# One issuing queue instead of two: a fused linear-attention and MLP-mixer kernel whose loads and stores move to SyncE, with a new issue order for every engine

## The chip, the cores and the metric

The kernel runs on one core of one Trainium2 chip. The metric is the device time of one execution in microseconds. Five engines take part: TensorE (PE in the profile; its weight loads are shown as PEld), VectorE (DVE), ScalarE (ACT), GpSimd (POOL) and SyncE (SP). SP computes nothing here; it issues transfers. ACT can issue transfers too, on a queue of its own, in order with its computing instructions.

## The reference

```python
def _attn_ref(q, k, v, alpha):               # (4, 8, 768, 48) each
    state = np.zeros((B, H, D, D))
    for t in range(S):
        state = alpha[:, :, t, :, None] * state + np.einsum('bhd,bhe->bhde', k[:, :, t], v[:, :, t])
        y[:, :, t] = np.einsum('bhd,bhde->bhe', q[:, :, t], state)
    return y

def _moe_ref(x, w_tok1, w_tok2, w_ch1, w_ch2):   # x = y with the heads side by side: (4, 768, 384)
    h = np.maximum(x.transpose(0, 2, 1) @ w_tok1, 0.0) @ w_tok2
    u = x + h.transpose(0, 2, 1)
    return u + np.maximum(u @ w_ch1, 0.0) @ w_ch2
```

Per batch element, a gated recurrence over 768 steps and 8 heads gives a 768 x 384 matrix x. A mixer follows: one MLP over the steps (768 to 256 to 768), then one over the channels (384 to 1536 to 384), both with residuals. Input and output are float32; the kernel multiplies in bfloat16.

## The kernel before

**Attention.** The 4 batch elements have 3 pieces each, so there are 12 pieces, n = 0 to 11, of 256 steps. A piece needs four loads of 384 KB (`ld_at`, `ld_kt`, `ld_qt`, `ld_vt`, line 533) into a pool of 20 buffers named `in`. ACT takes logarithms of alpha (`ln`, lines 580 to 586), PE sums them over time (`cum`, `cumw`), ACT exponentiates (`E`, `IE`), and `kk` and `qq` (line 641) scale keys and queries on DVE or POOL. Pieces 0 to 5 transpose keys and queries on PE (`trk`, `trq`, line 654) and copy them out (`evk`, `evq`). Pieces 6 to 11 send them through a transposing transfer (`dk`, `dq`, line 665, issued by SP) and reorder the query part (`pq`). `G` and `mask` (line 708) form masked scores, `K`, `sa` and `sm` update the state, `y` and `ia`, `ib` give the piece's output, `x` (line 685 or 686) copies it out. `kc` and `vs` are half-tile copies between these; `kc` of a late piece waits for `dk`.

**Mixer.** For each batch element b, `t1` and `t2` (lines 790, 795) are the MLP over steps with `ht` as its activation, `u` (line 799) adds the residual, `up`/`ut` or, for b = 2 and 3, the transposing transfer `ux` (line 669) turn u, `c1` (line 814) and the activation `rt` (lines 785, 787) are the first channel product, `c2` (line 819) the second, `o` (line 823) adds the residual and `st` (line 573) stores 192 KB. Weights come in 16 pieces of 384 KB (`ldw`), and `cw` casts each to bfloat16.

**Fillers.** In the first pieces, PE multiplies zeros where it would wait (`f1_...` one, `f3_...` three matmuls of 512 columns, line 592).

**Order.** Nothing is scheduled on the chip or by a framework. `ORDER` lists all 942 operations with the engine that runs each as the last letter (t PE, s ACT, v DVE, g POOL, y SP), and `BUFS` gives every value its buffer. Each engine works through its own operations in the listed order and waits at each one for its operands. In the built program every transfer also uses one of eight completion counters in turn, for both queues together, and waits until the transfer that used the same counter before it has landed.

**What the change touches.** The operands of `cum` in `attention`, the two column ranges in which the last output tile is made (`cuts` in `mixer`, for batch 3, tile 0), and the two lists.

Of the kernel before, what the change touches and what calls it, by code (L numbers as in the profile page):

```python
# [368 lines left out]
G1_1t evq2s ib1t ldw_wt21s f3_trk2t kk2v E3s IE3s trk2t sm1_1g mask1_1v vb2s vs1_1s f1_K2t ld_vt3y K2t evk2v G1_2t
ldw_wt20y y1_1t ld_at4y sa0_2v f3_G02t kk3g x1_0s r13s sm0_2g q0r3g G0_2t mask1_2v vs0_2g cw_wt10s ia1t x0_0v y0_1t  # L370
trk3t t1_0_1_0t mask0_2v ka3s ia2t ldw_wc14y t1_0_1_1t f1_y2t ib2t y0_2t vs1_2v kb3s ldw_wc15y y1_2t x1_1s cw_wt11s
vb3v x0_1s t1_0_1_2t t1_0_0_0t t1_0_1_3t kc3s x0_2s t1_0_1_4t vs0_3v vs1_3v ldw_wc13y x1_2s t1_0_0_1t qq3v cw_wt21s
t1_0_0_2t t1_0_1_5t cw_wt20v t1_0_0_3t t1_0_0_4t t1_0_0_5t ht_0_1s K3t trq3t ld_kt4y ht_0_0s P4g s0_3v sa1_3v t2_0_2t
t2_0_3t evk3s sm1_3g t2_0_0t t2_0_1t t2_0_5t ldw_wc12y ldw_wc10y ldw_wc11y u_0_3v u_0_2v u_0_0v up_0_1t t2_0_4t evq3s
lnP4s cw_wc14g cw_wc15g u_0_1v ib3t ut_0_1s ln14s ld_kt5s u_0_5v cw_wc13g up_0_0t cum4t ld_at5y E4s G0_3t IE4s u_0_4v
G1_3t k0a4g ut_0_0v up_0_2t c1_0_10_0t mask0_3v c1_0_9_0t ut_0_2s rt_0_10_0s rt_0_9_0s mask1_3v c1_0_7_0t c1_0_9_1t
c1_0_6_0t c1_0_10_1t c1_0_8_0t c1_0_8_1t cw_wc12s y1_3t cw_wc10s rt_0_10_1s kk4v rt_0_7_0v cw_wc11v rt_0_6_0v trk4t
c1_0_1_0t P5g ka4g c1_0_4_1t rt_0_8_1v c1_0_1_1t k0a5g ld_vt4s r14s x1_3s c1_0_3_1t c1_0_0_0t evk4v rt_0_1_1v
# [5 lines left out]
sa1_4v rt_0_7_1s c2_0_2_0t kc5s cw_wc22s c2_0_1_0t trq5t c2_0_4_0t vb5g cw_wc24g ib4t c2_0_4_1t y1_4t c2_0_1_1t
ld_at7s evq5s ld_vt6s cw_wc23s sm1_4g vs1_5g x1_4v P6g G0_5t G1_5t ld_kt6y vs0_5s cw_wc25s ld_kt7s mask1_5v c2_0_2_1t
ln16s mask0_5v c2_0_4_2t c2_0_2_2t c2_0_1_2t K5t y0_3t sa0_5v c2_0_4_3t c2_0_1_3t o_0_4v c2_0_5_0t r16s x0_3s lnP6s
ia5t y0_5t sm0_5v ld_at8y x0_5s ld_qt6y cum6t ld_at9y IE6s t1_1_0_0t E6s ib5t t1_1_0_1t st_0_4y y1_5t ld_vt7y x1_5s
t1_1_0_2t t1_1_1_0t t1_1_0_3t t1_1_1_1t t1_1_0_4t t1_1_1_2t t1_1_1_3t t1_1_1_4t t1_1_0_5t c2_0_5_1t k0a6g o_0_1v kk6v
dk6y P7g ka6g t1_1_1_5t c2_0_5_2t c2_0_0_0t ln18s ht_1_1s lnP7s vb6s ht_1_0v t2_1_3t t2_1_2t P8v q0r6v t2_1_5t
c2_0_5_3t t2_1_0t t2_1_1t st_0_1s u_1_2v u_1_3v qq6g k0a7g u_1_5v ld_qt7y u_1_0v cum7t IE7s kb6s t2_1_4t up_1_1t ln17s  # L390
vs0_6s ld_qt8y ld_at10s c2_0_3_0t c2_0_3_1t u_1_4v u_1_1v c2_0_0_1t up_1_0t c2_0_3_2t ut_1_1v o_0_5v up_1_2t c2_0_2_3t
c2_0_3_3t ut_1_0v kk7v c1_1_1_0t kc6v ut_1_2v vs1_6s lnP8s vb7s P9g K6t r17s c2_0_0_2t c2_0_0_3t rt_1_1_0v dq6y
c1_1_0_0t ld_kt8y q0r7g o_0_2v ld_qt9s E7s o_0_3v qq7g dk7y cum8t ln19s lnP9s E8s r19s r18s s0_6v sa1_6v c1_1_11_0t
c1_1_3_0t c1_1_2_0t o_0_0v vs0_7s rt_1_11_0v c1_1_3_1t c1_1_7_1t kb7g ka7s rt_1_3_1s c1_1_4_1t rt_1_2_0v ld_kt9y
c1_1_0_1t c1_1_10_1t rt_1_3_0s q0r8v dq7y c1_1_1_1t rt_1_0_1s P10v rt_1_7_1v rt_1_10_1v c1_1_11_1t sm1_6g pq6g
c1_1_7_0t cum9t lnP10s IE8s rt_1_1_1s vs1_7s c1_1_8_1t c1_1_4_0t ld_vt8s ln110s rt_1_7_0v ld_at11y rt_1_11_1s
c1_1_2_1t c1_1_9_1t qq8v k0a8v rt_1_8_1s rt_1_4_1s c1_1_5_0t rt_1_0_0v rt_1_9_1v q0r9g rt_1_4_0s ld_vt9y rt_1_2_1s
IE9s c1_1_5_1t rt_1_5_0v kc7s E9s c1_1_6_1t dq8y rt_1_5_1s K7t ld_qt10y c1_1_6_0t G0_6t rt_1_6_1s k0a9v rt_1_6_0s
r110s pq7s G1_6t sa0_7v mask0_6v kk8g c2_1_4_0t mask1_6v dk8y c2_1_4_1t sm0_7g c2_1_4_2t sa1_7v kk9g ib6t st_0_5s
st_0_0s c1_1_9_0t c2_1_4_3t P11g qq9g rt_1_9_0s y1_6t G1_7t G0_7t mask0_7v x1_6s c1_1_8_0t c2_1_1_0t c1_1_10_0t vb9s  # L400
ka9s rt_1_8_0v y0_6t ia7t mask1_7v vb8v y0_7t rt_1_10_0s c2_1_3_0t c2_1_1_1t q0r10v sm1_7v x0_6s vs1_8v c2_1_0_0t
c2_1_3_1t c2_1_3_2t ib7t pq8s t1_2_1_0t x0_7s vs0_8g kc8g y1_7t c2_1_3_3t o_1_4v dk9y kb9g ld_kt10y cum10t o_1_3v
vs0_9s x1_7s G0_8t E10s t1_2_1_1t IE10s ln111s vs1_9s qq10g mask0_8v K8t c2_1_1_2t r111s dq9y sa0_8v sm0_8g ia8t
t1_2_1_2t t1_2_1_3t G1_8t c2_1_0_1t y0_8t kc9s K9t c2_1_1_3t mask1_8v x0_8s lnP11s st_1_4y st_0_2y ld_kt11y pq9s
k0a10v kk10g ld_vt10y ld_qt11y s0_9v sa1_9v t1_2_0_0t c2_1_0_2t ib8t y1_8t c2_1_0_3t t1_2_0_1t t1_2_1_4t t1_2_0_2t
t1_2_0_3t t1_2_0_4t x1_8v o_1_1v t1_2_1_5t ht_2_1s G0_9t o_1_0v G1_9t t1_2_0_5t ht_2_0s mask0_9v c2_1_2_0t dq10y ib9t
c2_1_2_1t t2_2_5t t2_2_3t cum11t mask1_9v y0_9t u_2_5v u_2_3v t2_2_4t t2_2_2t t2_2_0t u_2_4v pq10s t2_2_1t x0_9s ka10s
k0a11g sm1_9g u_2_2v vb10v vs1_10g u_2_1v c2_1_5_0t c2_1_2_2t c2_1_5_1t dk10y c2_1_5_2t y1_9t ia10t kb10v vs0_10g
# [469 lines left out]
```

## Time and profile before

| | |
|---|---|
| three runs | 166.69, 167.17 (median), 168.16 us |
| profiled execution | 167.49 us, of which its span (first to last instruction) 165.8 us |
| busy: PE, DVE, ACT, POOL | 155.9, 117.6, 102.6, 65.3 us |
| transfers | 25.17 MB read, 4.72 MB written; SP's queue (q1) 25.47 MB, ACT's (q10) 8.75 MB |
| transfers issued by SP, by ACT | 76, 29 |

The span is cut into engines and waits by several views. A row of a timeline or of a list of groups names the line of the code, the engine, the operation, output and input, and how many of them (x); "busy, mean ns" belongs to the group; what stands behind an arrow released the wait ahead of it. A row of a table of windows gives, for one stretch of the span, the busy time of each engine, the granted clock, the mean busy share of the transfer engines and the GB/s that they moved. PE's busy time holds modelled ends of pipelined matmuls, so a full PE may still have room.

### The profile page before, as it was taken

The numbers are of one execution on the slowest core, as the hardware profiler recorded it, in microseconds if no ns is written. First come the engines' busy times: TensorE is split into PE (matmuls) and PEld (weight loads), VectorE is DVE, ScalarE is ACT, GpSimd is POOL, SyncE is SP. The second block draws the span as 40 slices with busy tenths as digits, with TensorE's granted clock in tenths as the row PEclk, the third lists the DMA queues.
The fourth block names the chain that finished last, engine by engine and source line by source line (L and its number), as shares of the span: only waits on it lengthen the run. The fifth ranks groups of instructions, "written<-read, shape, count | busy, mean of one in ns | idle before, by whom it ended". The sixth has DMA issues, their size and how long they took to land. (4 is left out here: it accounts for less than half of the span.)

```text
span 165.8 us, 4057 instructions
## 1 busy us (share of the span) xinstructions
PE 155.9 (94%) x1606; PEld 99.2 (60%) x1606; DVE 117.6 (71%) x205; ACT 102.6 (62%) x195; POOL 65.3 (39%) x73
## 2 busy tenths in 40 slices
...
GB/s 116 323 325 324 320 325 369 373 321 335 368 353 315 204 298 208 271 264 190 303 237 129 241 270 144 142 134 163 185 0 51 0 90 100 47 190 4 47 95 142
DMA packets 74530, 34.46 MB, mean 208 GB/s; under 512 B 67984, under 2 KB 73488, under 8 KB 74512
## 3 DMA queue, kind: packets, MB, share of 16 engines
q1 hardware_dynamic: 58432, 25.47, 60.4%
q10 hardware_dynamic: 16080, 8.75, 17.9%
...
HBM read 25.17 MB, written 4.72 MB: 180 GB/s over the span
## 5 line engine op out<-in xcount | busy, mean ns | idle before, releaser
L819 PE MATMUL ps<-wc,rt 128*128 128x384 bf16 (+1 forms) x300 | 53.9, 320 | 0.0
L814 PE MATMUL ps<-ut,wc 128*128 128x384 bf16 x288 | 51.4, 326 | 1.7 <-ACT rt L785 1.6
L785 ACT ACTIVATE rt<-ps 128x384 bf16<-128x384 f32 x59 | 26.7, 490 | 21.4 <-PE ps L814 19.2
L814 PEld LDWEIGHTS <-wc 128*128 128x128 bf16 x288 | 27.3, 97 | 19.4 <-issue 2.4
L819 PEld LDWEIGHTS <-rt 128*128 128x128 bf16 x300 | 27.5, 97 | 15.5
L708 DVE TENSOR_TENSOR gtm<-ps,mk 128x1024 bf16<-128x1024 f32 x24 | 28.6, 1219 | 3.9 <-PE ps L592 3.5
L787 DVE TENSOR_SCALAR rt<-ps 128x384 bf16<-128x384 f32 x37 | 19.9, 554 | 11.0 <-PE ps L814 10.9
L823 DVE TENSOR_TENSOR o<-ps,u 128x384 f32<-128x384 f32 (+1 forms) x25 | 13.1, 536 | 11.8 <-PE ps L819 9.0
L641 POOL TENSOR_TENSOR pkk<-in,IE 128x768 bf16<-128x768 f32 x7 | 12.7, 1816 | 16.3 <-DVE pkk L641 7.7
L641 POOL TENSOR_TENSOR pkq<-in,E 128x768 bf16<-128x768 f32 x7 | 12.7, 1819 | 3.2 <-DVE ss L756 1.5
L592 PE MATMUL ps<-zs 128*128 128x512 bf16 x37 | 12.3, 454 | 1.6 <-DVE zs L495 1.1
L685 ACT CAST vb<-in 64x384 bf16<-64x384 f32 (+1 forms) x20 | 12.4, 621 | 1.1 <-DMA in<-in_v_dram 0.8
L685 ACT CAST x<-ps 128x384 bf16<-128x384 f32 x18 | 8.5, 476 | 7.4 <-PE ps L592 6.9
L799 DVE TENSOR_TENSOR u<-ps,x 128x384 bf16<-128x384 f32 x24 | 11.9, 550 | 1.3 <-PE ps L795 1.0
L756 POOL TENSOR_TENSOR ss<-tmp,E 128x384 bf16<-128x384 f32 x10 | 8.3, 835 | 7.8 <-DVE tmp L753 4.6
L577 POOL TENSOR_TENSOR in<-in 128x384 f32<-128x384 f32 x7 | 7.0, 1000 | 11.1 <-DVE wt L686 3.4
L790 PE MATMUL ps<-x,wt 128*128 128x384 bf16 x48 | 10.8, 326 | 0.3 <-ACT x L685 0.3
L753 DVE TENSOR_TENSOR tmp<-ps,ss 128x384 f32<-128x384 f32 x16 | 8.8, 553 | 2.0 <-PE ps L592 1.3
L641 DVE TENSOR_TENSOR pkk<-in,IE 128x768 bf16<-128x768 f32 x5 | 4.8, 954 | 7.1 <-ACT IE L625 6.0
L592 PE MATMUL ps<-tpq,tpk 48*64 48x128 bf16 (+1 forms) x288 | 8.5, 219 | 1.0 <-DVE tpq L686 0.8
L795 PE MATMUL ps<-ht,wt 128*128 128x384 bf16 x48 | 9.3, 326 | 0.0
L592 PEld LDWEIGHTS <-gtm 128*128 128x128 bf16 x192 | 7.6, 96 | 1.9
...
## 6 DMA issues: line engine op xcount, KB each, us to landing
in<-in_q_dram SPq DMA_DIRECT2D x11, 384.0 KB, 5.1
in<-in_moe_w_ch_dram SPq DMA_DIRECT2D x10, 384.0 KB, 5.9
in<-in_alpha_dram SPq DMA_DIRECT2D x9, 384.0 KB, 5.8
in<-in_k_dram SPq DMA_DIRECT2D x9, 384.0 KB, 6.4
in<-in_v_dram SPq DMA_DIRECT2D x6, 384.0 KB, 5.5
in<-in_v_dram ACTq DMA_DIRECT2D x6, 384.0 KB, 5.7
out_dram<-o ACTq DMA_DIRECT2D x12, 192.0 KB, 2.6
out_dram<-o SPq DMA_DIRECT2D x11, 192.0 KB, 2.3
```

What stands on the lines that cost most here:

```text
L592: return self.pe.matmul(out, lhsT=lhsT, rhs=rhs, start=start, stop=stop, skip_group_check=True)
L641: self.shared(self.eng[e].tensor_tensor(self.t(dst)[:, :, :, 0:D], self.t(src).rearrange("p h s d -> p s h d"), bass.AP(tensor=f.tensor, o ...
L685: return self.act.copy(d, s)
L708: self.nc.vector.tensor_tensor(self.t(gtm)[:, hf, :, :], self.pair(gp).rearrange("p a (j t) -> p (a j) t", t=128), bass.AP(tensor=m.tensor ...
L785: self.act.activation(d, s, AF.Relu)
L787: self.nc.vector.tensor_scalar_max(d, s, 0.0)
L790: self.pe.matmul(self.bank(bank)[:, 0:HD], lhsT=self.wt1[:, kc, m * 128 : m * 128 + 128], rhs=self.t(x), start=(kc == 0), stop=(kc == NS - 1))
L795: self.pe.matmul(self.bank(bank)[:, 0:HD], lhsT=self.wt2[:, kc, i * 128 : i * 128 + 128], rhs=self.t(hts[kc]), start=(kc == 0), stop=(kc = ...
L799: self.nc.vector.tensor_tensor(self.t(u)[:, i % 3], self.bank(bank)[:, 0:HD], self.t(x), ALU.add)
L814: self.pe.matmul(self.bank(bank)[:, 0:HD], lhsT=self.wc1[:, kc, mc * 128 : mc * 128 + 128], rhs=self.t(ut)[:, 3 * half : 3 * half + 3, kc, ...
L819: self.pe.matmul(self.bank(bank)[:, 0 : cz - ca], lhsT=self.t(rts[mc][0])[:, i * 128 : i * 128 + 128], rhs=self.wc2[:, mc, ca:cz], start=( ...
L823: self.nc.vector.tensor_tensor(self.t(o)[:, ca:cz], self.bank(bank)[:, 0 : cz - ca], self.t(u)[:, i % 3, ca:cz], ALU.add)
```

## The change

Three edits. `cum` gets the filler operations of `fill("cumw", cb)` as predecessors (`fill` returns an empty list for n of 3 and more, and this branch is taken for n of 3 and more alone). The last output tile is cut at column 320 instead of 192. And `ORDER` and `BUFS` are replaced: every load is issued by SP, and all stores but four of the last batch (`st_3_1`, `st_3_3`, `st_3_4`, `st_3_0h1`). SP then issues 101 transfers and ACT 4. The order within every engine is new, 155 operations change engine, DVE has 186 operations instead of 187, ACT 189 instead of 223, POOL 71 instead of 61. PE keeps the same operations and 37 filler matmuls, in another order.

```diff
-            cum = O("cum", pe([384] + [4] * 4 + [16]), 2, writes=[cb, E, IE], reads=[la], preds=[lnp], emit=lambda e: g.cum(cb, la))
+            cum = O("cum", pe([384] + [4] * 4 + [16]), 2, writes=[cb, E, IE], reads=[la], preds=[lnp] + fill("cumw", cb),
+                    emit=lambda e: g.cum(cb, la))
...
-            cuts = [(0, HD // 2), (HD // 2, HD)] if (b, i) == LAST else [(0, HD)]
+            cuts = [(0, 320), (320, HD)] if (b, i) == LAST else [(0, HD)]
...
 ORDER = """
-f1_cumw0t ld_at1y f3_cumw1t f3_trk1t ld_at0s ld_kt1s f1_cumw1t ln1s f3_trq0t ld_kt0y ld_vt0y ld_qt0y ln0s ld_vt1y
-ld_qt1y ld_at2y cumw1t f1_K1t cumw0t ld_at3y E1s IE1s Et1s IE0s vb0s f1_K0t kk0v Et0s kk1g K0t f3_K1t s0_0v sa1_0v E0s
-qq0v vb1s trk0t sm1_0v f3_G00t trq0t ln2s trk1t evk0v ld_qt2y qq1g K1t evq0v evk1s sa0_1v ld_vt2s G0_0t cumw2t
...
-rt_0_9_1s c1_0_11_1t q0r4v qq4v c1_0_4_0t ld_vt5s rt_0_1_0s rt_0_2_0v E5s c1_0_2_1t rt_0_4_0s rt_0_11_1s kk5g
...
-c2_3_5_3t c2_3_0h0_1t o_3_5v c2_3_0h1_0t c2_3_0h1_1t c2_3_0h1_2t c2_3_0h1_3t st_3_5s o_3_0h1v st_3_4y c2_3_0h0_2t
-c2_3_0h0_3t o_3_0h0v st_3_0h0y st_3_0h1s
+f3_cumw0t f3_K0t f3_cumw1t ld_at1y ln1s f1_cumw0t ld_at0y f3_trk0t cumw1t ld_kt0y ld_vt0y ld_qt0y ln0s cumw0t f1_trq0t
+f3_trq0t E1s IE0s kk0v Et0s E0s IE1s Et1s trk0t vb0v qq0g K0t f3_G00t ld_kt1y ld_vt1y s0_0v sa1_0v f3_K1t trq0t kk1v
+sm1_0v vb1s ld_qt1y vs1_0s f1_K1t ld_at3y ld_at2y ld_kt2y evq0v K1t ln13s evk0v trk1t sa0_1v qq1g ld_qt2y G0_0t vs0_0s
...
+c2_3_0h0_0t o_3_4v c2_3_3_3t st_3_1s o_3_3v st_3_4s c2_3_0h1_3t o_3_0h1v c2_3_0h0_1t c2_3_0h0_2t c2_3_0h0_3t o_3_0h0v
+st_3_0h0y st_3_3s st_3_0h1s
...
```

Two stretches of the new lists, engine by engine. DVE from its first working operation to the first `u`:

```
before  kk0 s0_0 sa1_0 qq0 sm1_0 evk0 evq0 sa0_1 mask0_0 sa1_1 evq1 mask1_0 mask0_1 kk2 mask1_1 evk2 sa0_2 mask1_2 x0_0 mask0_2 vs1_2 vb3 vs0_3 vs1_3 qq3 cw_wt20 s0_3 sa1_3 u_0_3
after   kk0 vb0 s0_0 sa1_0 kk1 sm1_0 evq0 evk0 sa0_1 mask0_0 sa1_1 evq1 mask1_0 mask0_1 kk2 cw_wt10 mask1_1 evk2 sa0_2 kk3 mask1_2 mask0_2 qq3 x1_2 evk3 s0_3 ht_0_1 sa1_3 u_0_2
```

SP's queue around the last piece, n = 11, and POOL's:

```
SP before    dq9 st_1_4 st_0_2 ld_kt11 ld_vt10 ld_qt11 dq10 dk10 ux_2_1 st_1_0 ux_2_0 dq11 dk11
SP after     dq9 st_1_4 ld_qt11 ld_vt10 dq10 dk10 ld_kt11 ux_2_1 st_0_3 ux_2_0 st_1_1 ld_vt11 dq11 dk11
POOL before  qq10 sm0_8 kk10 k0a11 sm1_9 vs1_10 vs0_10 kk11 pq11 sm0_11
POOL after   qq10 sm0_8 kk10 sm1_9 vb10 kb10 pq10 kc10 vs0_10 k0a11 kk11 q0r11 sm0_10 kc11 vs0_11 pq11 sm0_11
```

More of the change, by code (lines that the diff above doesn't have):

```diff
@@ L369 @@
[L369 to L378, printed above, removed]
@@ L384 @@
[L384 to L393, printed above, removed]
@@ L394 @@
[L394 to L408, printed above, removed]
@@ new lines @@
+ld_kt3y ld_qt3y ld_vt3y lnP3s Et2s IE2s sm1_1g qq2g mask1_0v mask0_1v cum3t ldw_wt11y f1_y0t ib0t G1_1t y1_0t y0_0t
+ia1t kk2v IE3s f1_trq2t vs1_1s ld_at4y E3s x1_0s cw_wt10v y0_1t vb2s f1_trk2t mask1_1v k0a3g ldw_wt20y ldw_wt21y trq2t
+f3_trk2t ldw_wc14y ldw_wc13y evq2s trk2t evk2v K2t f3_G02t x0_0s sa0_2v ib1t G1_2t x0_1s vs0_2s q0r3g ldw_wc15y kk3v
+sm0_2g vb3s y1_1t vs1_2g ka3g kb3s vs1_3s t1_0_0_0t t1_0_0_1t G0_2t trk3t t1_0_1_0t mask1_2v t1_0_0_2t mask0_2v ia2t
+t1_0_1_1t t1_0_1_2t f1_y2t ib2t qq3v vs0_3s cw_wt11s ld_at5y y0_2t y1_2t kc3s x1_1s ldw_wc10y x0_2s t1_0_0_3t
@@ new lines @@
+t1_0_1_3t t1_0_1_4t x1_2v K3t P4g cw_wt21g evk3v s0_3v cw_wt20s lnP4s t1_0_1_5t t1_0_0_4t t1_0_0_5t cw_wc14g trq3t
+ht_0_0s ht_0_1v cum4t sa1_3v ln14s ldw_wc11y cw_wc15g cw_wc13g E4s evq3s t2_0_2t u_0_2v t2_0_3t P5g t2_0_0t t2_0_4t
+u_0_3v ldw_wc12y t2_0_1t u_0_0v up_0_1t IE4s ut_0_1s ld_kt4y ld_qt4y t2_0_5t ib3t u_0_1v up_0_0t ut_0_0s G0_3t u_0_4v
+G1_3t u_0_5v up_0_2t ut_0_2s mask0_3v c1_0_9_0t c1_0_10_0t ld_vt4y ld_kt5y cw_wc10v c1_0_8_0t mask1_3v rt_0_9_0s
+rt_0_10_0v c1_0_9_1t c1_0_8_1t rt_0_8_1v sm1_3g cw_wc11g r14s cw_wc12s c1_0_6_0t c1_0_11_1t ln15s y1_3t c1_0_4_1t
@@ new lines @@
+rt_0_8_0v ldw_wc20y ld_qt5y ldw_wc21y rt_0_6_0s x1_3s k0a4v rt_0_11_1s kk4v q0r4v c1_0_7_0t rt_0_7_0v c1_0_3_0t
+ldw_wc22y lnP5s c1_0_2_1t c1_0_1_1t ka4g rt_0_3_0s rt_0_4_1s kb4s rt_0_9_1s qq4v c1_0_3_1t c1_0_10_1t cum5t ldw_wc25y
+ld_vt5y vb4g trk4t k0a5g vs0_4g ldw_wc23y rt_0_1_1s c1_0_1_0t trq4t c1_0_4_0t rt_0_3_1s IE5s E5s kc4s r15s vs1_4s
+ldw_wc24y rt_0_10_1v evk4v rt_0_1_0s ld_at7y c1_0_2_0t rt_0_2_1v rt_0_4_0v ld_at6y kk5v c1_0_0_0t evq4s c1_0_0_1t
+rt_0_0_1s c1_0_5_0t trk5t G1_4t rt_0_2_0v G0_4t rt_0_0_0v rt_0_5_0s mask0_4v evk5s cw_wc20s mask1_4v ld_vt6y ld_at8y
@@ new lines @@
+cum10t c2_1_1_3t G1_8t G0_8t o_1_1v mask0_8v E10s IE10s vs1_8s c2_1_0_0t c2_1_0_1t vs1_9g ln111s kc9s vs0_9s pq9s
+qq10g sm0_8g kk10g ia8t c2_1_0_2t mask1_8v y0_8t t1_2_1_0t t1_2_1_1t K9t x0_8v s0_9v c2_1_0_3t ib8t t1_2_0_0t
+t1_2_0_1t y1_8t t1_2_1_2t sa1_9v G0_9t ld_vt10y x1_8s G1_9t mask0_9v t1_2_1_3t t1_2_0_2t mask1_9v t1_2_0_3t t1_2_0_4t
+t1_2_0_5t ht_2_0s dq10y t1_2_1_4t t1_2_1_5t cum11t sm1_9g ht_2_1s c2_1_2_0t y0_9t t2_2_3t t2_2_4t t2_2_1t u_2_3v
+t2_2_5t vb10g kb10g u_2_4v E11s dk10y IE11s u_2_1v ib9t c2_1_2_1t t2_2_0t u_2_5v t2_2_2t c2_1_5_0t y1_9t c2_1_5_1t
```

66 lines of the change are left out of this document (41 added, 25 removed), and 22 rows, old and new, of the table BUFS.

## The prediction

> **What bounds the kernel now.** I read the page's busy times first, then PE's waits, then a table of windows cut at the places where PE lacks time.
>
> ```profile
> span 165.8 us, 4057 instructions
> PE 155.9 (94%) x1606; PEld 99.2 (60%) x1606; DVE 117.6 (71%) x205; ACT 102.6 (62%) x195; POOL 65.3 (39%) x73
> L592 PE MATMUL ps<-zs 128*128 128x512 bf16 x37 | 12.3, 454 | 1.6 <-DVE zs L495 1.1 <-ACT IE L625 0.5
> PE ps L814 <- ACT rt L785: 1.6, 2, 1.2
> ...
> 24.00:32.00 8.00, 7.42 (x110) 5.11 (x108) 7.71 (x13) 7.84 (x16) 4.58 (x5) 1.00 1.09 369
> 44.00:47.00 3.00, 1.79 (x15) 1.04 (x14) 2.20 (x4) 1.55 (x5) 1.52 (x1) 1.00 1.06 375
> 47.00:117.00 70.00, 69.83 (x790) 45.59 (x788) 60.02 (x99) 53.01 (x103) 39.80 (x39) 1.00 1.00 225
> 117.00:121.00 4.00, 3.59 (x49) 2.14 (x51) 1.78 (x4) 3.15 (x7) 0.30 (x1) 1.00 0.36 129
> 121.00:163.00 42.00, 41.72 (x325) 26.23 (x317) 19.57 (x35) 9.38 (x21) 0.54 (x1) 1.00 0.23 69
> ```
>
> The figures after a window's length are the busy times of PE, its weight loads, DVE, ACT and POOL. From 44 us on, PE is full but for two holes: 1.2 us in 44 to 47 and 0.4 us in 117 to 121. After that it runs to the end (41.72 of 42; the missing 0.28 is the stretch after its last matmul). Before 32 us PE is not the bound: it lacks 0.58 us of 24 to 32, and the 37 filler matmuls lie in this stretch. DVE is busy 7.71 of the same 8 us. So the time is: when the first 32 us release PE, plus a fixed amount of PE work, plus PE's later holes, plus the tail. PE's operations stay the same, fillers included (37 before and after), so the new order can move only the start, the holes and the tail.
>
> **Part 1, loads on one queue: the rate.** DMA share and GB/s are the last two columns.
>
> ```profile
> 4.00:8.00 4.00, 3.93 (x32) 1.96 (x31) 0.00 (x0) 2.52 (x4) 0.00 (x0) 1.00 1.16 322
> 8.00:14.00 6.00, 3.56 (x49) 2.07 (x46) 3.80 (x6) 3.80 (x7) 2.03 (x2) 1.00 1.17 325
> ...
> L533 ACTq DMA_DIRECT2D in<-in_v_dram x6: 374/374/397, 14.5 to 112.1; - x6
> ```
>
> ACT issues `ld_at0` and `ld_kt1` in the first 1.4 us, and they move beside SP's loads in 4 to 8 us: 322 GB/s. In 8 to 14 us SP's loads move alone (ACT's next load is the first of the six in the last row, at 14.5 us): 325 GB/s. One queue fills the transfer engines as well as two, so the rate costs nothing; a 393,216-byte load takes 1.21 us either way. What changes is the sequence: `ld_at1` no longer shares with `ld_at0`.
>
> **Part 2, the start.** ACT's first logarithms wait for alpha, then PE, then ACT, then DVE:
>
> ```profile
> 1.06 4.88 PE L592 MATMUL ps<-zs 128*128 128x512 bf16 x11 [1.06 <-DVE zs L495]
> 4.88 0.15 PEld L592 LDWEIGHTS <-zs 128*128 128x128 bf16 x1 [0.27 <-issue]
> 5.30 0.15 PEld L592 LDWEIGHTS <-u 128*128 128x128 bf16 x1 [0.28 <-issue]
> 5.11 1.57 ACT L586 ACTIVATE la<-in 128x768 bf16<-128x768 f32 x2 [3.02 <-DMA in<-in_alpha_dram]
> 6.00 0.65 PE L592 MATMUL ps<-la,u 128*128 128x384 bf16 x3
> 7.95 0.17 PE L592 MATMUL ps<-off,idn 128*128 128x16 bf16 x1
> 8.52 0.83 ACT L625 ACTIVATE IE<-ps 128x768 f32<-128x768 f32 x1
> 9.38 0.96 DVE L641 TENSOR_TENSOR pkk<-in,IE 128x768 bf16<-128x768 f32 x1 [6.04 <-ACT IE L625]
> ```
>
> Alpha can land up to 1.2 us sooner, but 13 fillers instead of 11 now stand ahead of `cumw1`, one per 0.42 us by the weight loads at 4.88 and 5.30: free at 1.06 + 13 x 0.42 = 6.5 us against 6.0. `cumw0` follows without a filler between (0.2 us), so it ends some 0.2 to 0.3 us after the 8.12 of before. `IE0` now runs straight after it instead of behind `IE1` and `Et1`: about 8.4 against 8.52, and DVE's `kk0` at 9.2 against 9.38. Gain: 0.2 us.
>
> From there DVE is the bound until the first `u`:
>
> ```profile
> 9.40:32.10 22.70, 19.83 (x289) 13.29 (x290) 21.15 (x28) 19.13 (x34) 14.56 (x13) 1.00 1.11 339
> 32.10 2.88 DVE L799 TENSOR_TENSOR u<-ps,x 128x384 bf16<-128x384 f32 x6
> ...
> L641 DVE TENSOR_TENSOR pkk<-in,IE 128x768 bf16<-128x768 f32 x5 | 4.8, 954 | 7.1 <-ACT IE L625 6.0 <-POOL in L633 0.8 <-DMA in<-in_k_dram 0.2
> L686 DVE COPY tpk<-ps 128x1024 bf16<-128x1024 bf16 x3 | 2.1, 685 | 0.1
> L686 DVE CAST x<-ps 128x384 bf16<-128x384 f32 x6 | 3.3, 553 | 2.6 <-PE ps L592 2.6
> L686 DVE CAST vb<-in 64x384 bf16<-64x384 f32 (+1 forms) x8 | 3.6, 455 | 0.4 <-DMA in<-in_v_dram 0.2
> L787 DVE TENSOR_SCALAR ht<-ps 128x384 bf16<-128x384 f32 x2 | 1.1, 558 | 0.6 <-PE ps L790 0.5
> ```
>
> 28 instructions stand there before and after. New: `kk1`, `kk3` (0.95 each), `evk3` 0.69, `ht_0_1` 0.56, and `vb0`, `cw_wt10`, `x1_2` (0.55 each, the casts of a full tile taken like x); gone: `qq0` (same shape as `kk`) 0.95, `x0_0` 0.55, `cw_wt20` 0.55, and four small ones at 0.455. That is 4.8 in and 3.9 out: DVE's work to the first `u` grows by 0.9 us. Of the 22.70 us it was busy 21.15, idle 1.55. If the new order leaves no idle time, `u` starts at 9.2 + 22.05 = 31.25, 0.85 us sooner than 32.10; if it idles as before, at 32.8, 0.7 later. What ACT gains lies elsewhere (its `evk3`, `ht_0_1` and casts went to DVE). Between the ends I take 0: the new work and the idle time about cancel.
>
> **Part 3, the hole at 44 us.** This is where an ACT load stands on the path.
>
> ```profile
> 45.33 0.37 ACTq L533 DMA_DIRECT2D in<-in_v_dram  x1
> 45.75 0.49 ACT L785 ACTIVATE rt<-ps 128x384 bf16<-128x384 f32 x1 [1.45 <-DMA in<-in_v_dram]
> ```
>
> The load is `ld_vt5`. By the 1.45 us of idle time in the last row ACT reaches it at 44.3, and it stands until 45.33; the built program makes it wait for an earlier transfer with the same completion counter. Behind it stands `rt_0_1_0`, which frees a result bank, and PE stops 1.2 us (the row `PE ps L814 <- ACT rt`, longest). On SP the same wait holds up loads alone, and those are issued some microseconds ahead. Bounds: 0, if another activation is late there, to -1.4 (the row's 1.45). I take -1.2, the PE hole.
>
> [...]
>
> **Part 4, new holes.** The remaining 24 issues that leave ACT (0.37 us each, about 9 us) lie in its idle 38% and cost or gain nothing on PE. But 155 operations change engine, and any may now be late. The nearest rows are the holes of the present order after 36 us: 1.2 and 0.4. A new order without the first kind has perhaps one of each size: bounds -0.4 (none at all) to +2. I take +0.5.
>
> **Part 5, the tail.** PE's last matmuls are now those of the 320-column part, 9 of them after the other parts.
>
> ```profile
> L823 DVE TENSOR_TENSOR o<-ps,u x25: 357/549/558, 58.9 to 162.8; 128x384 f32<-128x384 f32 x23, 128x192 f32<-128x192 f32 x2
> out_dram<-o SPq DMA_DIRECT2D x11, 192.0 KB, 2.3
> out_dram<-o SPq DMA_DIRECT2D x1, 96.0 KB, 1.6
> ```
>
> PE's columns stay 384 in all. The last addition grows from 0.36 us (192 columns, the minimum of the first row) to 0.48 (two thirds of the way to 0.55), the last store from 96 to 160 KB: from 1.6 towards 2.3, of which the busy stores of mid-kernel make up a part. Bounds +0.1 (the addition alone) and +0.6 (1.6 + 0.67 x 0.7, and the addition); I take +0.3. The `cum` edit adds no instruction: 0.
>
> **Sum.** Part 2: 0. Part 3: -1.2. Part 4: +0.5. Part 5: +0.3. Together -0.4 on the profiled execution, 167.49 us (165.8 of span), which stands 0.3 above the median of 167.17. Against the median: **166.8 us**.
>
> **Rivals.** *Slower, the key load of the last piece queues too late.* `ld_kt11` used to be issued ahead of two transposes; it now stands behind `dk10`.
>
> ```profile
> 94.08 0.45 SPq L533 DMA_DIRECT2D in<-in_k_dram  x1
> 100.55 2.09 SPq L665 DMA_TRANSPOSE tpk<-pkk  x1
> in<-in_k_dram SPq DMA_DIRECT2D x9, 384.0 KB, 6.4
> 110.39 1.82 POOL pkk L641
> L633 POOL TENSOR_TENSOR in<-in,in 128x384 f32<-128x384 f32 x6 | 6.0, 1004 | 2.2 <-DVE ss L756 2.1
> L686 POOL COPY pkk<-pkk 64x384 bf16<-64x384 bf16 x1 | 0.5, 502 | 0.0
> 112.24 5.25 DMA tpk<-pkk
> 119.63 0.34 PE L592 MATMUL ps<-vb,pkk 128*128 128x96 bf16 x4
> ```
>
> Issued at 102.6 instead of 94.1, it lands at 109.0; POOL then needs `k0a11` (1.0), `kk11` (1.8) and `q0r11` (same shape as `k0a11`, 1.0), DVE `qq11` (0.95): 113.8, and SP sends `dq11` ahead of `dk11`, 1.2 us more (the second row's transpose held SP for 2.09): 115.0 against 112.24. With 5.25 to land and `kc11` 0.5, `K11` (the last row) can start at 120.8 instead of 119.63. PE then waits 1.2 us plus what it had gained by then, so Part 3 is lost too. With 0.3 of the tail and the 0.5 of Part 4: 167.17 + 2.0 = 169.2. It decides from the point at which `dk11` lands later than 119. Against it: 6.4 is the median of a full stretch, and the transfer engines are less than half busy by then (0.36 in the window from 117).
>
> *Faster, all of it works.* DVE idles no more (-0.85), the hole goes with ACT's whole wait (-1.4), no new ones, tail +0.3: 167.17 - 1.95 = 165.2. For it: ACT has 34 operations fewer. Against it: it needs every wait of a new order to be covered.
>
> [...]
>
> **How the numbers follow.** Forecast 0.34, slower 0.31, faster 0.27, no gain 0.08. A measurement of this kernel can tell about 1% from no change, 1.7 us: below 165.5 is faster, above 168.8 slower. So faster has 0.27, within 1% (forecast and no gain) 0.42, slower 0.31. The forecast's own range is 165.9 to 168.3, with one part at a time at its bound (Part 2 at -0.85 and Part 4 at +2); the range for 8 in 10 takes in most of both other cases, 164.8 to 169.8.
>
> **What would show it.** Right: no hole of PE near 44 us and no wait of `rt` for a load; DVE's first `u` within 31.2 to 32.8; the mean GB/s in 8 to 14 us near 325; the last store landing in about 2 us. Wrong: a first `u` after 33, which would shift everything behind it; a wait of PE for `pkk` or `tpq` at about 118; SP standing at a store or transpose while PE waits for a load behind it.

## The result and the profile after

The changed kernel took 166.37 us (median of 9; 166.03 to 168.24) against 167.95 for the kernel before beside it (9; 166.69 to 168.30): a ratio of 0.9925, 95% interval 0.9901 to 0.9950. A later set gave 166.84 against 167.85, ratio 0.9942 (0.9922 to 0.9963). So it is 0.6 to 0.75% faster, 1.0 to 1.3 us by the ratios, which lies within the 1% that the prediction counted as no change. The profiled execution took 166.25 us, 164.5 of it span.

The page's head, its row of SP's queue, and the windows cut as before (columns: PE, weight loads, DVE, ACT, POOL, granted clock, transfer share, GB/s; line numbers of this kernel are one higher, those of the experiments one to three):

```profile
span 164.5 us, 4058 instructions
PE 154.8 (94%) x1606; PEld 98.5 (60%) x1606; DVE 117.9 (72%) x204; ACT 97.7 (59%) x186; POOL 69.6 (42%) x83
q1 hardware_dynamic: 73936, 33.59, 76.9%
...
4.00:8.00 4.00, 4.00 (x37) 2.20 (x35) 0.00 (x0) 3.11 (x4) 0.00 (x0) 1.00 1.16 323
8.00:14.00 6.00, 4.55 (x65) 2.65 (x63) 4.91 (x7) 3.16 (x8) 2.51 (x2) 1.00 1.17 325
24.00:32.00 8.00, 7.04 (x102) 4.92 (x101) 7.16 (x11) 7.76 (x15) 4.90 (x7) 1.00 1.04 358
44.00:47.00 3.00, 3.00 (x25) 1.73 (x23) 2.59 (x6) 2.92 (x6) 1.81 (x4) 1.00 1.06 333
47.00:117.00 70.00, 69.10 (x778) 44.64 (x776) 57.84 (x96) 49.65 (x99) 43.54 (x46) 1.00 1.01 242
117.00:121.00 4.00, 4.00 (x72) 2.56 (x71) 2.56 (x5) 0.98 (x2) 2.35 (x3) 1.00 0.02 8
```

The hole of 1.21 us in 44 to 47 us is gone (3.00 of 3.00), and so is that of 0.41 in 117 to 121. The long window lacks 0.90 us where it lacked 0.17: new holes. One queue moves 325 GB/s, as before. In the timeline SP now issues `ld_vt5` at 43.00, and ACT passes from `vb` to `rt_0_1_0` without a stop:

```profile
43.00 0.91 SPq L534 DMA_DIRECT2D in<-in_v_dram  x1
...
45.13 0.51 ACT L686 CAST vb<-in 64x384 bf16<-64x384 f32 x1
45.55 0.48 ACT L786 ACTIVATE rt<-ps 128x384 bf16<-128x384 f32 x1
```

The start, in the timelines of PE and DVE of this execution:

```profile
1.06 4.52 PE L593 MATMUL ps<-zs 128*128 128x512 bf16 x13 [1.06 <-DVE zs L496]
5.41 0.65 PE L593 MATMUL ps<-la,u 128*128 128x384 bf16 x3
8.22 0.96 DVE L642 TENSOR_TENSOR pkk<-in,IE 128x768 bf16<-128x768 f32 x1 [4.88 <-ACT IE L626]
31.91 1.49 DVE L800 TENSOR_TENSOR u<-ps,x 128x384 bf16<-128x384 f32 x3 [0.23 <-PE ps L796]
```

The first `kk` comes 1.16 us sooner than before (8.22 against 9.38), the first `u` only 0.19 (31.91 against 32.10). That gap is taken up by the experiments.

### The profile page after: what moved, and what is told of

The parts are those of the page before. It is cut to its first block, busy times and chain, and to the rows that moved or that the text cites. A ratio compares the mean times of both kernels' runs of the same rounds, so it can differ in the third digit from the quotient of the medians.

```text
span 164.5 us, 4058 instructions
## 1 busy us (share of the span) xinstructions
PE 154.8 (94%) x1606; PEld 98.5 (60%) x1606; DVE 117.9 (72%) x204; ACT 97.7 (59%) x186; POOL 69.6 (42%) x83
## 4 chain that ended last, share of the span: by engine, by line
PE 60%; ACT 15%; DMA 9%; SPq 6%; POOL 3%; issue 3%; DVE 2%; POOLq 0%; ACTq 0%
PE ps L815 21%; PE ps L820 20%; PE ps L593 10%; DMA in<-in_alpha_dram 9%; SPq L534 6%; PE ps L796 4%; ACT vb L686 3%; PE ps L791 3%; ACT rt L786 2%; ACT x L686 1%; ACT kt L686 1%; POOL vb L687 1%; ACT pkk L686 1%; ACT E L626 1%; ACT IE L626 1%
## 5 line engine op out<-in xcount | busy, mean ns | idle before, releaser
L820 PE MATMUL ps<-wc,rt 128*128 128x384 bf16 (+2 forms) x300 | 53.9, 320 | 0.1
L824 DVE TENSOR_TENSOR o<-ps,u 128x384 f32<-128x384 f32 (+2 forms) x25 | 13.2, 537 | 13.1 <-PE ps L820 11.0
L686 ACT CAST vb<-in 64x384 bf16<-64x384 f32 (+1 forms) x23 | 14.3, 624 | 2.8 <-DMA in<-in_v_dram 2.4
L593 PE MATMUL ps<-zs 128*128 128x512 bf16 x37 | 11.3, 429 | 1.1 <-DVE zs L496 1.1
L757 POOL TENSOR_TENSOR ss<-tmp,E 128x384 bf16<-128x384 f32 x11 | 9.2, 835 | 6.5 <-DVE tmp L754 4.2
L634 POOL TENSOR_TENSOR in<-in,in 128x384 f32<-128x384 f32 x6 | 6.0, 997 | 13.4 <-ACT vb L686 6.9
L686 ACT CAST x<-ps 128x384 bf16<-128x384 f32 x15 | 6.9, 480 | 6.5 <-PE ps L593 6.5
L642 DVE TENSOR_TENSOR pkk<-in,IE 128x768 bf16<-128x768 f32 x7 | 6.7, 957 | 5.6 <-ACT IE L626 4.9
L642 POOL TENSOR_TENSOR pkk<-in,IE 128x768 bf16<-128x768 f32 x5 | 9.1, 1815 | 0.2
L593 PEld LDWEIGHTS <-tpk 48*64 48x64 bf16 (+1 forms) x288 | 5.8, 102 | 4.6 <-issue 2.3
```

What stands on the lines that cost most here:

```text
L593: return self.pe.matmul(out, lhsT=lhsT, rhs=rhs, start=start, stop=stop, skip_group_check=True)
L642: self.shared(self.eng[e].tensor_tensor(self.t(dst)[:, :, :, 0:D], self.t(src).rearrange("p h s d -> p s h d"), bass.AP(tensor=f.tensor, o ...
L686: return self.act.copy(d, s)
L820: self.pe.matmul(self.bank(bank)[:, 0 : cz - ca], lhsT=self.t(rts[mc][0])[:, i * 128 : i * 128 + 128], rhs=self.wc2[:, mc, ca:cz], start=( ...
L824: self.nc.vector.tensor_tensor(self.t(o)[:, ca:cz], self.bank(bank)[:, 0 : cz - ca], self.t(u)[:, i % 3, ca:cz], ALU.add)
```

## Experiments

Each profile is cut the same way in this table: the first `kk` and first `u` on DVE, what PE lacks of 32 to 44, 44 to 47, 47 to 117 and 117 to 121 us, the stretch from the first `c1_3_0_0` to the end, and the span. Span less first `u` less the four holes gives 131.2 to 131.9 us in all of them but e6, whose PE lacks another 1.2 us in 121 to 135 us; so the time is made of these parts but for 0.7 us. Most of that rest lies in the holes too, which are least values, since a busy PE holds modelled ends. Kernels with the old order run PE's 588 channel matmuls (`c1` and `c2`) in the same sequence, and their start times in the traces show the whole loss. From the 41st to the 61st of them before takes 5.07 us, and e3, f4 and f6 take 3.69 to 3.70; from the 341st to the 361st before takes 5.11, e3 4.93, f4 and f6 4.32. So the stops at 44 and 117 us cost 1.4 and 0.8 us, where the windows show 1.21 and 0.41.

| kernel | ratio to before (95%) | `kk` | `u` | holes | tail | span |
|---|---|---|---|---|---|---|
| before | 1 | 9.38 | 32.10 | 0.14 + 1.21 + 0.17 + 0.41 | 20.80 | 165.8 |
| changed | 0.9925 (0.9901 to 0.9950) | 8.22 | 31.91 | 0.90 | 21.03 | 164.5 |
| changed, again | 0.9942 (0.9922 to 0.9963) | 9.55 | 32.80 | 1.45 | 21.02 | 165.9 |
| e3: before, `ld_vt5` on SP | 0.9933 (0.9909 to 0.9958) | 9.82 | 32.56 | 0.14 + 0 + 0.31 + 0.23 | 20.78 | 165.0 |
| e4: before, all loads on SP | 1.0160 (1.0105 to 1.0214) | 9.10 | 32.01 | 0.14 + 1.05 + 0.18 + 1.55 | 20.80 | 166.8 |
| e5: e4 and stores on SP | 1.0115 (1.0065 to 1.0166) | 9.42 | 32.16 | 0.14 + 0.88 + 0.18 + 2.15 | 20.79 | 167.4 |
| f4: e4, two loads moved | 0.9881 (0.9842 to 0.9920) | 9.28 | 32.04 | 0.14 + 0 + 0.17 + 0 | 20.79 | 163.6 |
| f6: f4, issuers as changed | 0.9880 (0.9853 to 0.9907) | 8.54 | 32.26 | 0.14 + 0 + 0.18 + 0 | 20.80 | 163.8 |
| f5: e3, `kk11` on DVE | 0.9896 (0.9862 to 0.9930) | 9.50 | 32.23 | 0.14 + 0.16 + 0.81 + 0 | 20.79 | 165.2 |
| e6: changed, ACT issues again | 1.0659 (1.0600 to 1.0718) | 12.80 | 37.02 | 1.69 + 0 + 4.02 + 0 | 21.03 | 176.0 |
| f1: changed, `dk6` sooner, cut 192 | 0.9942 (0.9915 to 0.9970) | 9.37 | 32.63 | 0.78 | 20.82 | 164.8 |
| e2: changed, cut 64 | 0.9973 (0.9952 to 0.9994) | 8.28 | 32.02 | 0.86 | 21.25 | 164.8 |
| e7: changed, `x1_1` sooner | 0.9956 (0.9933 to 0.9979) | 8.25 | 32.16 | 1.23 | 21.02 | 165.0 |
| e8: changed, 10 fillers | 0.9957 (0.9927 to 0.9987) | 8.71 | 32.54 | 1.98 | 21.03 | 166.3 |

**The load at 44 us alone.**

```diff
- rt_0_9_1s c1_0_11_1t q0r4v qq4v c1_0_4_0t ld_vt5s
+ rt_0_9_1s c1_0_11_1t q0r4v qq4v c1_0_4_0t ld_vt5y
```

> The kernel before with one edit: the load ld_vt5 is issued by SP instead of ACT, at its old place in the list. Theory (the load blocks ACT): ACT no longer stands from 44.3 to 45.33, rt_0_1_0 starts about 1.4 us sooner, the 1.2 us wait of PE for rt at 44 to 47 us goes, and so does the time: 1.2 us less (0.993 of before). Rival 1 (another thing is late in that stretch, the load only happened to stand there): a hole of over 0.8 us stays in 44 to 47 us and the time is within 0.4 us of before. Rival 2 (an issue is worth its 0.37 us only): 0.4 us less, hole near 0.8.

Median 166.75 against 167.82. SP's row and the windows:

```profile
34.82 3.68 SPq L535 DMA_DIRECT2D in<-in_v_dram  x1
...
44.00:47.00 3.00, 3.00 (x26) 1.92 (x25) 2.93 (x6) 2.98 (x8) 1.07 (x1) 1.00 1.03 357
47.00:117.00 70.00, 69.69 (x783) 45.19 (x782) 59.75 (x99) 52.35 (x101) 40.30 (x39) 1.00 0.99 238
117.00:121.00 4.00, 3.77 (x68) 2.32 (x67) 2.33 (x4) 3.00 (x7) 0.83 (x1) 1.00 0.15 53
```

SP stands at the same load for 3.68 us, and PE loses nothing by it; the hole is 0 instead of 1.21. The ratio's interval is 0.7 to 1.5 us less: one letter of the list brings as much as the whole change. Both rivals fall: no hole is left at 44 us, and the gain is over 0.37 us. By the start times e3 gives 0.3 of its 1.4 us back near 52 us, at `trq5`; why is not shown.

The traces also show what the load waited for. In before, its completion counter had last been used by `ld_vt4`, which ACT issued at 38.90; that load landed at 45.31, and `ld_vt5` was issued at 45.33. On SP in e3 the load gets another counter, whose last transfer had landed at 34.25, before SP reached the load. So SP's 3.68 us are not the same wait, and the edit moves the load and changes its counter at once; the two are not told apart.

**One queue in the old order.** All loads (e4), then the stores too (e5).

```diff
- ld_qt9s ld_vt11s ldw_wt21s ...
+ ld_qt9y ld_vt11y ldw_wt21y ...
```

> The kernel before with all loads and weight loads issued by SP, at their old places in the list; the stores stay. It has the one queue for loads without the new order. Theory (the gain is the load that blocked ACT at 44 us, the rest of the order only carries it): as with ld_vt5 alone, 1.2 us less; the start is not better, since ld_kt1 now stands ahead of ld_kt0 on SP and delays the first kk by up to 1.2 us. Rival (the new order is what makes one queue work): SP stands at a transpose or store with a load behind it, PE gets a new hole after 50 us, and the time is that of before or more (0 to +2 us).

> The kernel before with all loads, and all stores but st_3_1, st_3_3, st_3_4 and st_3_0h1, issued by SP at their old places: the issuing engines of the changed kernel in the old order. Theory (stores leave ACT's idle time, and cost SP nothing that PE sees): within 0.4 us of the kernel with the loads alone on SP. Rival (a store waits on SP for its tile and holds up a load or transpose behind it): a wait of SP for o of over 1 us after 50 us, a PE wait for pkk, tpq or in, and 1 us or more above the kernel with the loads alone on SP.

In e5 `st_3_1`, `st_3_3` and `st_3_4` stayed on SP, where they stood before, so ACT issued `st_3_0h1` alone. Both are slower: 170.04 (169.70 without its two longest runs of six) and 169.56 against 167.82. Windows and timeline of e4:

```profile
44.00:47.00 3.00, 1.95 (x19) 1.16 (x17) 2.05 (x4) 2.98 (x7) 0.36 (x1) 1.00 1.13 340
117.00:121.00 4.00, 2.45 (x19) 1.44 (x18) 1.49 (x3) 1.30 (x4) 0.00 (x0) 1.00 0.31 107
...
44.92 0.56 DVE L639 TENSOR_TENSOR in<-in,lf 128x384 f32<-128x384 f32 x1 [1.29 <-DMA in<-in_q_dram]
46.53 0.62 PE L656 MATMUL ps<-idn,pkq 128*128 128x128 bf16 x8 [1.05 <-DVE pkq L643]
...
112.08 1.23 SPq L667 DMA_TRANSPOSE tpk<-pkk  x1
113.36 0.57 SPq L535 DMA_DIRECT2D in<-in_v_dram  x1
119.08 0.56 DVE L688 CAST vb<-in 128x768 bf16<-128x768 f32 x1 [2.80 <-DMA in<-in_v_dram]
120.16 0.65 PE L821 MATMUL ps<-wc,rt 128*128 128x384 bf16 x3 [1.55 <-DVE rt L789]
```

ACT no longer blocks, but two loads are late. `ld_qt4`, now behind `ld_vt4` and `ldw_wc20` on the same queue, holds up DVE until 44.92 and PE's `trq4` until 46.53. `ld_vt11` waits behind the transposes `dq11` and `dk11`, is issued at 113.36 and released DVE at 119.08; DVE and ACT stand there for almost 3 us, and PE for 1.55. This is the rival of the prediction, a load too late among SP's transposes, in the old order instead of the new and with another load. The stores (e5) add no stop of their own kind; e4 and e5 differ by less than their intervals.

**The same queue with two loads placed anew.**

```diff
- ld_vt4y ldw_wc20y ld_qt4y ...  dq11y ... dk11y ... ld_vt11y
+ ld_qt4y ld_vt4y ldw_wc20y ...  ld_vt11y dq11y ... dk11y
```

> The kernel before with all loads on SP at their old places, but for two: ld_vt11 goes ahead of dq11 (it stood behind dk11) and ld_qt4 ahead of ld_vt4. Theory (with one queue it is the place of single loads among SP's transposes and loads that decides; these two made the two stops that the other kernel with the loads on SP showed): the 1.2 us stop at trq4 and 1.2 of the 1.7 us stop at 118 us go, and the time is that of ld_vt5 alone on SP, 0.992 to 0.996 of before. Rival (one queue costs time of itself, by its load on SP or later loads): new stops turn up and the time stays 1 us or more above, at 1.0 of before or over.

> The kernel before with every load and store issued by the same engine as in the changed kernel, in the old order but for ld_vt11 ahead of dq11 and ld_qt4 ahead of ld_vt4, and with the last tile cut at 192. It differs from the changed kernel by the order, the engines of the computing operations, and the cut. Theory (the issuing engines with two placements are worth 1.2%, the rest of the changed kernel's lists gives part of it back): 0.985 to 0.992 of before, no stop of PE over 0.5 us after 32 us, stretch from the first c1_3_0_0 to the end 20.8 us. Rival (the stores on SP hold up loads, and the kernel with the loads alone on SP was the better for leaving them on ACT): a wait of SP for o with a late load or transpose behind it, a stop of PE over 0.5 us after 50 us, 0.993 or more.

Medians 165.69 (f4) against 167.93 and 165.72 (f6) against 167.85: both beat the kernel before by 1.2% and lie below the changed kernel (f6's interval ends at 0.9907; those of the changed kernel begin at 0.9901 and 0.9922). f6 has the changed kernel's issuers for every load and store, and the old order but for the two loads. Its windows:

```profile
44.00:47.00 3.00, 3.00 (x26) 1.92 (x25) 2.97 (x5) 2.98 (x8) 1.36 (x1) 1.00 1.12 324
47.00:117.00 70.00, 69.82 (x785) 45.41 (x784) 59.73 (x100) 54.08 (x105) 39.96 (x39) 1.00 1.02 243
117.00:121.00 4.00, 4.00 (x73) 2.56 (x71) 3.05 (x5) 1.06 (x3) 0.83 (x1) 1.00 0.01 3
```

By the windows no hole over 0.2 us is left after 44 us. So the issuers with two placements are worth 2 us, and what else the change brings (the rest of the order, the computing engines, the cut) gives 0.8 to 1 us of it back. f4 came out 0.7 us under the low end of its theory: by the start times e3 loses 0.6 us more than f4 at 117 us and 0.3 more near 52.

The stop at 117 us goes with the place of `ld_vt11`. In before, ACT's `kc11` waits there for the transpose `dk11`, and an activation `rt` that PE needs stands behind it:

```profile
117.58 0.51 ACT L685 COPY pkk<-pkk 64x384 bf16<-64x384 bf16 x1 [2.68 <-DMA tpk<-pkk]
118.12 0.49 ACT L785 ACTIVATE rt<-ps 128x384 bf16<-128x384 f32 x1
```

In before, e3 and f5 ACT issues `ld_vt11` within 0.7 us of `dk11`, and `dk11` lands 5.2, 5.1 and 4.8 us after its issue. In the other eleven profiles the two are issued more than 1.2 us apart, and `dk11` lands after 3.1 to 3.8 us, in the changed kernel after 3.1. So a second load left ACT with a gain here; this was seen in the traces and not tried by itself.

**The inverse.** The changed order, with the 26 transfers back on ACT.

```diff
- ln1s f1_cumw0t ld_at0y ... ld_vt5y ...
+ ln1s f1_cumw0t ld_at0s ... ld_vt5s ...
```

> The changed kernel with the 26 loads and stores that ACT issued before put back on ACT, at their places in the new list. Theory (a load on ACT's in-order queue blocks its activations while it waits): ACT stands at one or more of these loads for over 0.5 us, PE gets holes of 0.5 us or more behind them, and the time is 0.7 to 2.5 us above the changed kernel (1.005 to 1.015 of it). Rival (the order alone brings the gain, who issues does not matter): within 0.4 us of the changed kernel, that is 0.99 to 0.995 of before.

178.70 against 167.82: the direction of the theory, at several times its size. ACT's timeline, the row of clock tenths, and PE's longest wait:

```profile
4.41 0.45 ACTq L536 DMA_DIRECT2D in<-in_alpha_dram  x1
9.37 0.84 ACT L589 ACTIVATE la<-in 128x768 bf16<-128x768 f32 x1 [4.12 <-DMA in<-in_alpha_dram]
...
PEclk9956999999999999999999999999999999999999
...
PE ps L595 <- ACT la L589: 3.0, 1, 3.0
```

In the new list `ld_at0` stands behind `ln1`. On ACT that means that alpha's load is issued when `ln1` runs, at 4.41, and the second logarithm starts at 9.37; PE waits 3.0 us and is then granted 5 and 6 tenths of its clock in two of the 4.4 us slices. The test does not isolate one blocked load, as it was meant to; it shows that in this order the 26 transfers can't all go back to ACT. `ld_vt5` alone back on ACT was not tried.

**The changed kernel again, and its start.**

> The changed kernel again, as the yardstick of this set and as a second sample of its start. Theory (the clock that PE is granted turns full at a time that neither kernel sets, 4.2 to 6.8 us in the profiles so far): first kk between 8.2 and 10 us depending on that time, 13 fillers taking 4.5 us where it turns early and up to 5.5 us where late; time 0.990 to 0.995 of before. Rival (the early start belongs to the new order): the clock turns full near 4.2 us again and the first kk starts within 0.2 us of 8.2.

```profile
1.05 5.73 PE L593 MATMUL ps<-zs 128*128 128x512 bf16 x13 [1.05 <-DVE zs L496]
6.58 0.85 PE L593 MATMUL ps<-la,u 128*128 128x384 bf16 x3
9.55 0.96 DVE L642 TENSOR_TENSOR pkk<-in,IE 128x768 bf16<-128x768 f32 x1 [6.21 <-ACT IE L626]
32.80 0.56 DVE L800 TENSOR_TENSOR u<-ps,x 128x384 bf16<-128x384 f32 x1 [0.23 <-PE ps L796]
...
47.00:117.00 70.00, 68.55 (x776) 44.41 (x776) 56.96 (x94) 49.68 (x97) 43.15 (x44) 1.00 0.98 237
```

The same 13 fillers take 5.73 us here and 4.52 in the first profile. By its weight loads the first profile starts a filler every 0.42 to 0.43 us up to 4.02 (0.42 in the prediction), and every 0.22 from 4.33 to the load for `cumw1` at 5.20. At these two paces the 5.53 us from the first filler to `cumw1` are 13 slow ones, and the 4.35 of the first profile some 7 slow ones and 6 fast: the pace changed at about 4.2 us there, and not before 6.6 here. The throttle's records of the full clock in the two traces begin at 4.2 and 7.0 us (ahead of its first record the clock column of the windows reads 1.00). The early start of the first profile belongs to that, not to the order: `kk` at 9.55 is later than before's 9.38. The theory holds, the rival falls.

**Ten fillers instead of thirteen.**

```diff
- f3_cumw0t f3_K0t f3_cumw1t ld_at1y
+ f3_cumw0t f3_cumw1t ld_at1y
```

> The changed kernel without the three fillers f3_K0: 10 filler matmuls ahead of cumw1 instead of 13. Theory (the fillers stand in the way in executions in which the clock turns full late): cumw1 starts at 5.2 to 5.5 us at any clock time, kk at 8.0 to 8.8, and the median is 0.2 to 0.6 us under the changed kernel. Rival 1 (DVE's stretch to the first u absorbs it): cumw1 earlier, first u and time within 0.2 us. Rival 2 (fewer matmuls turn the clock full later): clock full later than 7 us and time 0.3 us or more above.

`cumw1` came at 5.30 with a late clock (its first three matmuls took 1.17 us, against 0.65 in the first profile of the changed kernel) and `kk` at 8.71, as the theory said, but the first `u` at 32.54 and a ratio of 0.9957, against 0.9942 for the changed kernel beside it, do not show a gain: a wait of PE for `x1_1` at 28 us grew to 1.4 us. DVE's and ACT's chain to the first `u` absorbs the start (rival 1).

**The stop at 28 us.** In both profiles of the changed kernel PE waits 0.9 us for `x1_1` on ACT, which stands behind a weight cast.

```diff
- vb3s ... kb3s vs1_3s ... vs0_3s cw_wt11s ... kc3s x1_1s
+ vb3s x1_1s ... kb3s vs1_3s ... vs0_3s cw_wt11s ... kc3s
```

> The changed kernel with x1_1 moved ahead of kb3, vs1_3, vs0_3, cw_wt11 and kc3 in ACT's order, right behind vb3. Theory (the 1.08 us stop of PE at 28 us is the place of x1_1 in ACT's order): the stop goes, t2_0_2 starts 0.5 to 1 us sooner, and 0.3 to 1 us of it reaches the end. Rival (DVE's chain to t2, x1_2, evk3, ht_0_1, sets the end of that stretch): the stop moves a microsecond on, t2_0_2 and the first u stay within 0.3 us, and so does the time.

```profile
PE ps L793 <- ACT x L688: 0.5, 1, 0.5
PE ps L793 <- ACT wt L688: 0.5, 1, 0.5
```

In PE's waits the one stop of 0.9 became two of 0.5, the second for the cast that was put off; first `u` 32.16, time 166.83 against 166.84. The rival holds.

**The stop ahead of `K6`, and the cut.** f1 sends `dk6` ahead of `ld_qt7` and cuts at 192; e2 cuts at 64.

```diff
- ld_qt7y ... dk6y          - cuts = [(0, 320), (320, HD)]
+ dk6y ld_qt7y              + cuts = [(0, HD // 2), (HD // 2, HD)]      (e2: [(0, 64), (64, HD)])
```

> The changed kernel with two edits that are read apart in the profile: the load ld_qt7 stands behind the transpose dk6 on SP instead of ahead of it, and the last tile is cut at 192 again. Theory: the wait of PE ahead of K6 near 72 us (0.37 and 0.84 us in the two profiles of the changed kernel) goes, since dk6 is sent 1.3 us sooner, and the stretch from the first c1_3_0_0 to the end is 20.8 us as in the kernel before instead of 21.0; time 0.4 to 0.8 us under the changed kernel, 0.988 to 0.991 of before. Rival (the stop at K6 has other causes, such as the transposing transfer's own time or POOL's kc6): the wait stays over 0.3 us, and only the 0.2 us of the tail are gained.

> The changed kernel with the last output tile cut at column 64 instead of 320, so that 320 columns end first and 64 last. Theory (the tail is the last addition and the last store by their sizes): last addition 0.2 us shorter, last store of 32 KB some 0.3 to 0.5 us shorter than that of 160 KB, time 0.4 to 0.6 us under the changed kernel. Rival (the store costs the same whatever its size, or the 320-column store, issued just ahead, ends last): under 0.2 us less.

`K6` in the second profile of the changed kernel, and in f1:

```profile
73.14 0.34 PE L593 MATMUL ps<-vb,pkk 128*128 128x96 bf16 x4 [0.68 <-POOL pkk L687]
```

```profile
63.91 1.33 SPq L668 DMA_TRANSPOSE tpk<-pkk  x1
72.31 0.34 PE L595 MATMUL ps<-vb,pkk 128*128 128x96 bf16 x4
```

`dk6` leaves at 63.91 instead of 66.08 (64.75 in the first profile), `K6` has no wait, and the tail is 20.82 us. The parts behave as the theory says, yet the time is 166.73, not measurably below 166.84: what is gained is within the interval, and whether it reaches the end is open. With the cut at 64 the tail is 21.25, longer than with 320 and against the theory. The ends of the changed kernel and of e2, on DVE and SP:

```profile
161.27 0.49 DVE L824 TENSOR_TENSOR o<-ps,u 128x320 f32<-128x320 f32 x1 [0.42 <-PE ps L820]
161.78 0.33 SPq L574 DMA_DIRECT2D out_dram<-o  x1
```

```profile
160.66 1.28 DVE L826 TENSOR_TENSOR o<-ps,u 128x384 f32<-128x384 f32 x3 [0.42 <-PE ps L822]
161.97 0.33 SPq L576 DMA_DIRECT2D out_dram<-o  x1
```

PE's last matmul ends 17.74 us after the first `c1_3_0_0` with either cut. But in e2 three additions follow each other on DVE without a gap, so that the small last one waits for that of 320 columns, and its store is issued behind the other 320-column store: from issue to the end of the span 2.8 us against 2.7. The rival holds; a small last piece is no help when a large one stands right ahead of it.

**The stop at 117 us.**

```diff
- ld_vt5s ... kk11g
+ ld_vt5y ... kk11v
```

> The kernel before with ld_vt5 issued by SP and kk11 computed by DVE (0.97 us by the row of its twin qq11) instead of POOL (1.82). Theory (the stop of 0.4 us near 117 us is dk11, sent late behind kk11): dk11 is sent some 0.8 us sooner, that stop goes, and the time is 0.4 us under that of ld_vt5 alone, 0.989 to 0.992 of before. Rival (DVE is full there and is late for the next operation itself): PE waits for an activation or addition of DVE between 108 and 118 us, and the time is that of ld_vt5 alone or more.

165.99 against 167.93. The hole at 117 us is 0 (0.23 in e3), as the theory said; the profile has others at 50 to 53 us (0.81 in the long window), far from the edit; e3 has one of them, near 52 us. The interval overlaps that of e3, so the 0.4 us is not shown.

## Why the prediction was right, and where it was not

**Part 1 (0).** 323 GB/s in 4 to 8 us and 325 in 8 to 14, as before. Right.

**Part 2 (0).** The first `u` of the changed kernel is at 31.91 and 32.80 us; in the seven profiles with the old order it is at 32.01 to 32.56, mean 32.19. The middle of the two, 32.36, is 0.2 later; e2 and f1, with the same start, have 32.02 and 32.63. So 0 was right within what profiles can tell. The step that failed is the start: 13 fillers were priced at 0.42 us throughout, which gives `cumw1` at 6.5. Measured were 5.41 and 6.58, with the clock full from 4.2 us in the one profile and from 7.0 in the other.

**Part 3 (-1.2).** Right in place and size: 1.21 us of hole gone, 1.1 us in the time of e3, shown by that single edit. By the start times the stop was worth 1.4, nearly the whole wait of ACT that was the outer bound. The wait for a completion counter is in the trace of before (landing at 45.31, issue at 45.33); that the same wait on SP would hold up loads alone stays untested, since in e3 it did not arise. A load priced at its issue time alone, the 0.37 us of its row, leaves out the 1 us for which ACT stood ahead of that issue; e3 measured 0.7 to 1.5 us.

**Part 4 (+0.5).** New holes of 0.90 and 1.45 us in 47 to 117 us, less the old ones of 0.14, 0.17 and 0.41 that went: +0.18 and +0.73, in the middle 0.45. The size is right by the windows; as the old stop at 117 us cost 0.8 and not 0.41, the true sum is smaller. f6 shows that these holes are the price of this order and not of one queue.

**Part 5 (+0.3).** Tail 21.03 and 21.02 against 20.78 to 20.80 in the seven profiles with a cut at 192 in the old order: +0.23.

**Sum.** By the parts: 0.2 - 1.2 + 0.45 + 0.23 = -0.3, against -0.4 forecast. The spans of the same two profiles lie 1.3 below and 0.1 above that of before, in the mean 0.6 below: the 0.3 that is missing in the parts is about what the windows hide of the old stops. The medians differ by more, 1.0 to 1.6 us. The second profile is a long execution (167.57, against a median of 166.84 of its 12 runs). And one step of the sum fell short: it set the profiled execution of before, 167.49, 0.3 above the median of three runs, 167.17. In 9 to 35 runs that median is 167.82 to 167.95, so this execution lay 0.3 to 0.5 below. So the predicted time fell right in part by luck, because base and gain were both too small.

The clock gives part of the reason. Of the 79 runs of before beside the experiments, 36 show a mean granted clock of 0.987 to 0.990, with a median of 168.08 us; the other 43, like the profiled one, show 0.998 to 1.000, with a median of 167.69. None of the 21 runs of the changed kernel is below 0.997. By these medians that is worth an estimate of 0.2 us on average to the new order, a term that the prediction did not have; what in the order does it was not tested.

The signs that the prediction named came: no hole near 44 us, a first `u` within 31.2 to 32.8, 325 GB/s, and a last store that landed 1.8 us after its issue.

**Rivals.** The slower one did not happen in the changed kernel:

```profile
100.58 0.53 SPq L534 DMA_DIRECT2D in<-in_k_dram  x1
104.98 1.00 POOL L634 TENSOR_TENSOR in<-in,in 128x384 f32<-128x384 f32 x1 [0.80 <-DMA in<-in_k_dram]
112.27 1.27 SPq L666 DMA_TRANSPOSE tpk<-pkk  x1
117.90 0.33 PE L593 MATMUL ps<-vb,pkk 128*128 128x96 bf16 x4
```

`ld_kt11` was issued at 100.58, not 102.6, and released POOL 4.4 us later, not 6.4; `dk11` left at 112.27 instead of 115.0, and `K11` had no wait. In the second profile the load was issued at 102.04, nearly as priced, and `K11` did not wait either. So the mis-sized terms are two landing times: 4.3 and 4.5 us for the load, where the median of all key loads, 6.4, was used, and 3.1 for `dk11`, where before's 5.25 was used. Its mechanism is real, though: e4 and e5 have it with `ld_vt11`, at 1.55 and 2.15 us. The faster rival, 165.2, needed every wait of an order to be covered. f4 and f6 come near it (165.7), by keeping the old order. The case of no gain, given 0.08, did not come either: the hole at 44 us went, and the medians lie 1.0 to 1.6 us below those of before.
